# Convolution by FFT and mixture of experts on one core: inverse and unfolded loads in 64x64 tiles

## The chip, the cores and the metric

The kernel runs on one core of a Trainium2 chip. The metric is device microseconds of one execution, as the median of several runs. A profile is of one execution of its own, and its span is a little shorter than that execution's time.

## What is computed

For each of 8 sequences x of 5056 positions and 128 channels, a causal convolution with a filter h of the same length, channel by channel, written in the reference as a product of spectra of twice the length. Every row of the result then goes through a mixture of experts: a group of 4 by the largest logit, one of that group's 4 experts by the largest logit, two matrices with a ReLU between them, weighted by both softmax values.

```python
def _attn_ref(x, h):
    L = 2 * S
    Yf = np.fft.rfft(x, n=L, axis=1) * np.fft.rfft(h, n=L, axis=0)[None, :, :]
    return np.fft.irfft(Yf, n=L, axis=1)[:, :S, :]
...
            h = np.maximum(xg[mask_e] @ w1[g, e], 0.0)
            ye = h @ w2[g, e]
            out[tok_idx] = combined[:, None] * ye
```

## The kernel before

The transform of L = 10112 points is split into 158 x 64. A position is n1 * 64 + n2; only 79 of the 158 values of n1 hold data. All of this part is FP32, and the work goes in three rounds of three "units" each: h with sequences 0 and 1, then 2 to 4, then 5 to 7.

- **Stage 1** (`stage1`, L371) of a round does the 158-point transform over n1, for 79 frequencies. It takes 48 loads of 8 channels each: a tile of 80 partitions (79 rows of x and one of zeros, laid so that the even rows of n1 lie in partitions 24 to 63 and the odd ones in 64 to 103) by 512 elements. The matrix `f` is the moving operand, x the stationary one. Two of three loads are **folded** (L419): even and odd rows are transformed apart, in four 64x64 tiles of the array, to 40 frequencies (80 columns), and ACT and DVE make sum and difference of the two. Every third load (`i % 3 == 2`) is **unfolded** (L426): all 128 partitions as the contraction, two column tiles of 128x64, 158 columns, and ACT alone copies the result (L443). A step of the program is half a load, with a pair of PSUM banks for each load. When a load is done its tile becomes free and up to two new transfers are issued (L450), from SP in round 0 and from ACT's queue in the other rounds.
- **Groups** (`groups`, L463) take the 79 frequencies in 40 pairs `p`, two pairs to a step, 20 steps and a tail. `forward` (L503, matmuls L520) does the 64-point transform over n2 in 64x64 tiles; DVE multiplies with the spectrum of h (L538, twice a pair); POOL (round 0) or DVE (rounds 1 and 2) adds the two products (L572); `inverse` (L576, matmuls L587) does the 64-point inverse of an earlier step's pairs: four matmuls of a 64x128 tile each, `w` = 256 columns in round 0 and 384 in the others; ACT copies the result (L597) and SP stores it to `zd` in device memory.
- **Side** (`side`, L684) does the last 158-point inverse for a finished round (L721, L735), transposes (L778), the gating on DVE, and scatters rows, sorted by expert, through POOL. It runs woven into stage 1 and the groups of the next round, and for the last round into the experts.
- **Experts**: blocks of 512 rows through both matrices, each product as three matmuls of 512 columns on high and low parts (L1350 to L1352, L1368 to L1370).

The order on each engine is written out by the program: `weave` places the steps of the side between the main steps by weights. Each engine works its own queue in that order and waits on semaphores. The gating's running sums over an expert's tokens are one scan (L937) of a matrix of ones and zeros, `smask`, [128, 240] in FP32, which DVE writes twice in the program (L747).

Of the kernel before, what the change touches and what calls it, by code (L numbers as in the profile page):

```python
# [9 lines left out]
F32 = mybir.dt.float32  # L10
F32R = mybir.dt.float32r
BF16 = mybir.dt.bfloat16
# [8 lines left out]
N1, N2 = 158, 64  # L21
# [44 lines left out]
LP = 2  # L66
# [28 lines left out]
def dft_constants():  # L95
# [7 lines left out]
    f = np.zeros((128, N1))  # L103
    f[X0:X0 + NH + 1] = rows
# [108 lines left out]
def columns(nu):  # L213

    n = 8 * nu * NH
    t = (n + GP - 1) // GP
    return t, n - (t - 1) * GP
# [11 lines left out]
class Kernel:  # L229
# [33 lines left out]
    def setup(self):  # L263
# [11 lines left out]
        self.f = cp.tile([128, N1], F32, name="f")  # L275
        nc.sync.dma_start(out=self.f, in_=a["c_f"])

    def setup2(self):
# [74 lines left out]
        self.smask = cp.tile([128, NE * columns(3)[0]], F32, name="smask")  # L353
# [17 lines left out]
    def stage1(self, r):  # L371
# [21 lines left out]
        def load(eng=nc.sync):  # L393
            if asked[0] >= len(loads) or not free:
                return
            i = asked[0]
            asked[0] += 1
            u, q = loads[i]
            b = ROUNDS[r][u]
            src = a["h"] if b < 0 else a["x"][b]  # L400
            held[i] = t = free.pop(0)
            eng.dma_start(
                out=t[X0:X0 + NH + 1].rearrange("p (d n) -> p d n", n=N2), in_=src[:, 2 * q * QB:2 * (q + 1) * QB, :]
            )
            tiles[i] = t.rearrange("p (i h n) -> p i h n", h=2, n=N2)

        def mm(k):
            i, h = k // 2, k % 2
            u, q = loads[i]
            fold = i % 3 != 2  # L410
# [3 lines left out]
            whole = pp.rearrange("p b c -> p (b c)")  # L414
            for j in range(h * QB // 2, (h + 1) * QB // 2):
# [8 lines left out]
                else:  # L424
                    for c in range(2):
                        nc.tensor.matmul(  # L426
                            whole[c * 64:c * 64 + 64, j * 256:j * 256 + N1], lhsT=tiles[i][:, j, c, :], rhs=self.f,
                            start=True, stop=True, tile_position=(0, c * 64),
                        )
# [33 lines left out]
    def groups(self, r):  # L463
# [112 lines left out]
        def inverse(p):  # L576
# [7 lines left out]
            for part in range(2):  # L584
                for c in range(n):
                    wt, k = (cgs[p + LP], 320 - part * 64) if p > 0 else (first[0], part * 128)
                    nc.tensor.matmul(  # L587
                        pz[c][:, 0:w], lhsT=wt[c * 64:c * 64 + 64, k:k + 128],
                        rhs=y[c * 64:c * 64 + 64, part, 0:w], start=part == 0, stop=part == 1,
                        tile_position=(c * 64, 0),  # L590
                    )
# [1146 lines left out]
```

## Time and profile before

| | |
|---|---|
| median of 3 runs | 1703.45 us (1699.97 to 1713.07) |
| the profiled execution | 1699.58 us, span 1697.9 us |
| TensorE's granted clock | 0.993 of full speed |
| TensorE busy | 96% of the span |
| VectorE, ScalarE, GpSimd busy | 77, 62, 46% |
| stage 1 of rounds 0, 1, 2 | to 52.5 us, 156 to 216, 372 to 453 us |
| groups of rounds 0, 1, 2 | 52.5 to 156, 216 to 372, 453 to 612 us |

The page gives busy shares of the span, the span in 40 slices, the DMA queues and the costliest groups of instructions. The timeline lists instructions in order of time, neighbours of one kind merged, with the idle time ahead of them and what ended it; "issue" stands for a wait that nothing in the profile explains. Matmuls overlap and their ends are modelled, so the distance between two starts says what a piece takes. An FP32 matmul of the program is two records on TensorE, each with a weight load.

### The profile page before, as it was taken

What the parts mean: (1) busy time and instruction counts of PE and PEld (TensorE: products, weight loads), DVE (VectorE), ACT (ScalarE), POOL (GpSimd) and SP (SyncE); (2) the same over time, 40 slices, a digit from 0 to 9 for tenths busy, and PEclk for the clock granted to TensorE, in tenths of its full rate; (3) what the DMA queues carried; (4) which work ended last, traced back from release to release, by engine and by line L of the source; (5) the groups of instructions that cost most, each with busy time, mean ns of one, the idle gap of its engine ahead of it and who ended that gap; (6) DMA issues with size and microseconds to landing.
All of it is one profiled execution on the core that took longest, in us unless ns stands there. A gap on an engine that the chain in (4) does not pass through costs nothing. (4 is left out here: it accounts for less than half of the span.)

```text
span 1697.9 us, 49029 instructions
## 1 busy us (share of the span) xinstructions
PE 1637.9 (96%) x17369; PEld 1287.7 (76%) x17369; DVE 1302.8 (77%) x3092; ACT 1047.2 (62%) x2461; POOL 773.4 (46%) x742
## 2 busy tenths in 40 slices
PE   8998999998999989999999999999999999999997
PEld 7666766657766657888888887888888888878987
DVE  6554689885688886777777788888887788787876
ACT  4554544544454456666666676677777776666765
POOL 1353234342465553254544554355555664243444
PEclk9999999999999999999999999999999999999998
DMA  7688778878799976565565544457555674445455
GB/s 207 204 266 247 204 218 265 271 249 216 195 282 294 292 235 185 164 179 166 169 176 170 170 137 137 150 179 227 160 155 171 189 242 127 131 125 155 153 162 157
DMA packets 277993, 330.23 MB, mean 194 GB/s; under 512 B 31863, under 2 KB 210304, under 8 KB 277720
## 3 DMA queue, kind: packets, MB, share of 16 engines
q1 hardware_dynamic: 248856, 270.93, 54.2%
q0 software_dynamic: 20608, 41.79, 7.2%
q10 hardware_dynamic: 8256, 14.10, 3.1%
q8 instruction: 144, 2.36, 0.6%
q14 instruction: 129, 1.06, 0.2%
HBM read 230.35 MB, written 96.86 MB: 193 GB/s over the span
## 5 line engine op out<-in xcount | busy, mean ns | idle before, releaser
L854 POOL DMA_INDIRECT srt<-rw,pos x320 | 345.7, 1080 | 388.8 <-DVE pos L853 112.4
L1421 POOL DMA_INDIRECT out<-orow,at x176 | 187.8, 1067 | 253.8 <-ACT at L1419 226.3
L538 DVE TENSOR_TENSOR y<-pp,hg 128x768 f32<-128x768 f32 (+1 forms) x120 | 103.7, 864 | 60.3 <-ACT hg L528 37.1
L1421 POOL DMA_INDIRECT out<-orow,sids x92 | 93.8, 1020 | 121.8 <-DVE orow L1388 85.5
L597 ACT COPY zs<-pp 128x768 f32<-128x768 f32 (+1 forms) x118 | 85.1, 721 | 84.7 <-PE pp L587 52.1
L587 PE MATMUL pp<-y,cg 64*128 64x384 f32 (+1 forms) x736 | 120.2, 456 | 9.9 <-DVE m L538 8.1
L1356 DVE SCALAR_TENSOR_TENSOR h0l<-px,h0h 128x512 fp32r<-128x512 f32 (+1 forms) x109 | 73.6, 676 | 59.4 <-ACT h0h L1355 58.5
L520 PE MATMUL pp<-st,cg 64*64 64x192 f32 (+1 forms) x1556 | 115.3, 407 | 0.5 <-PE pp L587 0.4
L1355 ACT ACTIVATE h0h<-px 128x512 fp32r<-128x512 f32 (+1 forms) x109 | 63.9, 586 | 80.8 <-PE px L1352 72.7
L438 DVE TENSOR_TENSOR st<-pp,odd 128x320 f32<-128x320 f32 x96 | 46.9, 489 | 76.6 <-ACT odd L437 74.3
L538 DVE TENSOR_TENSOR m<-pp,hg 128x768 f32<-128x768 f32 (+1 forms) x120 | 102.9, 858 | 2.2 <-ACT hg L530 2.2
L587 PEld LDWEIGHTS pp<-y,cg 64*128 64x128 f32 x736 | 68.2, 187 | 46.6 <-issue 16.8
L1356 DVE SCALAR_TENSOR_TENSOR h2l<-px,h2h 128x512 fp32r<-128x512 f32 (+1 forms) x112 | 75.6, 675 | 31.1 <-ACT h2h L1355 30.0
L742 ACT COPY yT<-py 128x474 f32<-128x474 f32 (+1 forms) x96 | 44.5, 514 | 77.0 <-PE py L735 76.9
L1356 DVE SCALAR_TENSOR_TENSOR h3l<-px,h3h 128x512 fp32r<-128x512 f32 (+1 forms) x111 | 74.6, 672 | 22.5 <-ACT h3h L1355 21.0
L520 PEld LDWEIGHTS pp<-st,cg 64*64 64x64 f32 x1556 | 56.1, 132 | 45.3 <-issue 34.9
L572 POOL TENSOR_TENSOR y<-y,m 128x512 f32<-128x512 f32 x40 | 50.8, 1274 | 83.4 <-DVE m L560 44.8
L721 PEld LDWEIGHTS py<-ig,zm 126*64 126x64 f32 x2048 | 73.2, 137 | 19.4 <-issue 6.8
L721 PE MATMUL py<-ig,zm 126*64 126x79 f32 x2048 | 80.7, 234 | 4.1 <-ACT rw L779 2.8
L1355 ACT ACTIVATE h3h<-px 128x512 fp32r<-128x512 f32 (+1 forms) x111 | 65.2, 587 | 29.1 <-PE px L1352 24.1
L1356 DVE SCALAR_TENSOR_TENSOR h1l<-px,h1h 128x512 fp32r<-128x512 f32 (+1 forms) x111 | 74.7, 673 | 4.2 <-ACT h1h L1355 0.3
L1355 ACT ACTIVATE h1h<-px 128x512 fp32r<-128x512 f32 (+1 forms) x111 | 65.2, 588 | 17.1 <-PE px L1352 14.7
(476 smaller groups left out, 5153.5 us busy)
## 6 DMA issues: line engine op xcount, KB each, us to landing
wr<-in_moe_w SPq DMA_DIRECT2D x373, 256.0 KB
zd<-zs SPq DMA_DIRECT2D x78, 384.0 KB
zm<-zd SPq DMA_DIRECT2D x64, 378.0 KB
cg<-in_c_g SPq DMA_DIRECT2D x102, 224.0 KB
xr<-srt SPq DMA_DIRECT2D x71, 260.0 KB
hg<-hd SPq DMA_DIRECT2D x80, 128.0 KB
zd<-zs SPq DMA_DIRECT2D x39, 256.0 KB
xt<-in_x ACTq DMA_DIRECT2D x54, 160.0 KB
```

Of the source, the lines that this page charges most:

```text
L438: nc.vector.tensor_tensor(out=all_st[:, 0:2 * HALF, d], in0=even, in1=odd, op=ALU.add)
L520: nc.tensor.matmul(px[c * 64:c * 64 + 64, b, to], lhsT=k, rhs=data[:, of], start=begin, stop=i == len(steps) - 1 or p == 0 and i == 1, til ...
L538: nc.vector.tensor_tensor(out=t[:, :, 0:w].rearrange("p t (r u d) -> p t r u d", r=2, u=nu), in0=taken(px, part).unsqueeze(1).broadcast_to ...
L572: (nc.gpsimd if r == 0 else nc.vector).tensor_tensor(out=y[:, :, 0:w], in0=y[:, :, 0:w], in1=m[:, :, 0:w], op=ALU.add)
L587: nc.tensor.matmul(pz[c][:, 0:w], lhsT=wt[c * 64:c * 64 + 64, k:k + 128], rhs=y[c * 64:c * 64 + 64, part, 0:w], start=part == 0, stop=part ...
L597: nc.scalar.copy(out=z[:, 0:n, 0:w], in_=pp[:, 0:n, 0:w])
L721: nc.tensor.matmul(pys[q][c:c + 64, col(n, u)], lhsT=zms[q][:, n % QB, k:k + 64], rhs=self.ig[:, 0:NH], start=n % QB == 0 and u == 0, stop ...
L742: nc.scalar.copy(out=self.yT[:, k:k + QB * c1], in_=pys.pop(q)[:, 0:QB * c1])
L854: ins = self.nc.gpsimd.indirect_dma_start(out=self.srt, out_offset=bass.IndirectOffsetOnAxis(ap=k["pos"][0:p, j:j + 1], axis=0), in_=k["rw ...
L1355: nc.scalar.activation(out=hh, in_=p, func=AF.Relu)
L1356: nc.vector.scalar_tensor_tensor(out=hl, in0=p, scalar=0.0, in1=hh.bitcast(F32), op0=ALU.max, op1=ALU.subtract)
L1421: ins = self.nc.gpsimd.indirect_dma_start(out=self.a["out"], out_offset=bass.IndirectOffsetOnAxis(ap=ids, axis=0), in_=o, in_offset=None, ...
```

## The change

- The **inverse** is cut along its 128 output rows: eight matmuls of a 64x64 tile for a pair in place of four of 64x128, in the order of half `h`, then frequency `c`.
- An **unfolded load** comes as two transfers. Channels 0 to 3 of the load go to the array's first half, partitions 24 to 63, and channels 4 to 7 to the second, 64 to 103; in each half the even rows of n1 lie first along the free dimension, the odd rows behind them. The contraction over 80 rows becomes two accumulating matmuls over 40, in four 64x64 tiles.
- `f` gets 158 more columns: the even and odd rows' coefficients with the halves exchanged.
- `smask` is held in bfloat16.

```diff
-    f = np.zeros((128, N1))
-    f[X0:X0 + NH + 1] = rows
+    f = np.zeros((128, 2 * N1))
+    f[X0:X0 + NH + 1, 0:N1] = rows
+    f[X0:X0 + HALF, N1:] = rows[HALF:]
+    f[X0 + HALF:X0 + 2 * HALF, N1:] = rows[:HALF]
...
-        self.smask = cp.tile([128, NE * columns(3)[0]], F32, name="smask")
+        self.smask = cp.tile([128, NE * columns(3)[0]], BF16, name="smask")
...
+            if folded(i):
+                eng.dma_start(
+                    out=t[X0:X0 + NH + 1].rearrange("p (d n) -> p d n", n=N2),
+                    in_=src[:, 2 * q * QB:2 * (q + 1) * QB, :],
+                )
+            else:
+                for b in range(2):
+                    d = 2 * q * QB + b * QB
+                    eng.dma_start(
+                        out=t[X0 + b * HALF:X0 + (b + 1) * HALF].rearrange("p (s d n) -> p s d n", s=2, n=N2),
+                        in_=src[:, d:d + QB, :].rearrange("(s p) d n -> p s d n", s=2),
+                    )
...
+            if not fold:
+                for s in range(2):
+                    for c in range(2):
+                        for b in range(2):
+                            j = b * QB // 2 + h
+                            nc.tensor.matmul(
+                                whole[c * 64:c * 64 + 64, j * 256:j * 256 + N1],
+                                lhsT=tiles[i][b * 64:b * 64 + 64, s * QB // 2 + h, c, :],
+                                rhs=self.f[b * 64:b * 64 + 64, (b + s) % 2 * N1:(b + s) % 2 * N1 + N1],
+                                start=s == 0, stop=s == 1, tile_position=(b * 64, c * 64),
+                            )
...
-                else:
-                    for c in range(2):
-                        nc.tensor.matmul(
-                            whole[c * 64:c * 64 + 64, j * 256:j * 256 + N1], lhsT=tiles[i][:, j, c, :], rhs=self.f,
-                            start=True, stop=True, tile_position=(0, c * 64),
-                        )
...
             for part in range(2):
-                for c in range(n):
-                    wt, k = (cgs[p + LP], 320 - part * 64) if p > 0 else (first[0], part * 128)
-                    nc.tensor.matmul(
-                        pz[c][:, 0:w], lhsT=wt[c * 64:c * 64 + 64, k:k + 128],
-                        rhs=y[c * 64:c * 64 + 64, part, 0:w], start=part == 0, stop=part == 1,
-                        tile_position=(c * 64, 0),
-                    )
+                wt, k = (cgs[p + LP], 320 - part * 64) if p > 0 else (first[0], part * 128)
+                for h in (0, 64):
+                    for c in range(n):
+                        nc.tensor.matmul(
+                            pz[c][h:h + 64, 0:w], lhsT=wt[c * 64:c * 64 + 64, k + h:k + h + 64],
+                            rhs=y[c * 64:c * 64 + 64, part, 0:w], start=part == 0, stop=part == 1,
+                            tile_position=(c * 64, h),
+                        )
```

The order of the engines' work stays; the number of instructions in its pieces changes. On TensorE at the start of stage 1 of round 0 (`pp` is the pair of PSUM banks, `xt` a tile of x, `f` the matrix; the shape is the output's, x16 the number of matmuls), before:

```order
L419 MATMUL pp<-f,xt_80 64x80 x16
L419 MATMUL pp<-f,xt_81 64x80 x16
L426 MATMUL pp<-f,xt_82 64x158 x8
L419 MATMUL pp<-f,xt_83 64x80 x16
L419 MATMUL pp<-f,xt_84 64x80 x16
L426 MATMUL pp<-f,xt_80 64x158 x8
```

and now:

```order
L444 MATMUL pp<-f,xt_80 64x80 x16
L444 MATMUL pp<-f,xt_81 64x80 x16
L434 MATMUL pp<-f,xt_82 64x158 x16
L444 MATMUL pp<-f,xt_83 64x80 x16
L444 MATMUL pp<-f,xt_84 64x80 x16
L434 MATMUL pp<-f,xt_80 64x158 x16
```

Every third load has 16 matmuls for 8; the others are as they were.

On TensorE in the groups of round 0, the second and third steps (`st` is stage 1's result, `cg` and `ns` the transform's matrices, `y` the product), before:

```order
L520 MATMUL pp_1166<-st_95,cg_909 64x384 x4
L520 MATMUL pp_1166<-st_95,cg_909 64x192 x4
L520 MATMUL pp_1166<-st_95,ns_1139 64x192 x4
L587 MATMUL pp_1191<-y_1106,first_716 128x256 x4
L587 MATMUL pp_1200<-y_1129,cg_909 128x256 x4
L520 MATMUL pp_1212<-st_95,cg_959 64x384 x4
```

and now:

```order
L539 MATMUL pp_1310<-st_95,cg_1024 64x192 x4
L539 MATMUL pp_1310<-st_95,ns_1283 64x192 x4
L607 MATMUL pp_1335<-y_1250,first_800 64x256 x8
L607 MATMUL pp_1348<-y_1273,cg_1024 64x256 x8
L539 MATMUL pp_1364<-st_95,cg_1079 64x384 x4
L539 MATMUL pp_1364<-st_95,cg_1079 64x192 x4
```

The inverse stands at its place with eight matmuls for four, of 64 output rows.

On ACT's queue in stage 1 of round 1 (`odd` and `st` are its copies out of PSUM, DMA rows the loads that it issues), before:

```order
L443 COPY st<-pp 128x158x4
L402 DMA xt_81<-in_x 80x512
L437 COPY odd<-pp 128x320
L402 DMA xt_82<-in_x 80x512
L437 COPY odd<-pp 128x320
L402 DMA xy<-in_x 80x512
```

and now:

```order
L462 COPY st<-pp 128x158x4
L412 DMA xt_81<-in_x 40x2x256 x2
L456 COPY odd<-pp 128x320
L405 DMA xt_82<-in_x 80x512
L456 COPY odd<-pp 128x320
L405 DMA xy<-in_x 80x512
```

An unfolded load is two commands of 40 partitions for one of 80, at the same place.

More of the change, by code (lines that the diff above doesn't have):

```diff
@@ L274, in setup @@
             nc.vector.memset(t, 0.0)
-        self.f = cp.tile([128, N1], F32, name="f")
+        self.f = cp.tile([128, 2 * N1], F32, name="f")
         nc.sync.dma_start(out=self.f, in_=a["c_f"])
@@ L401, in load, with folded @@
             held[i] = t = free.pop(0)
-            eng.dma_start(
-                out=t[X0:X0 + NH + 1].rearrange("p (d n) -> p d n", n=N2), in_=src[:, 2 * q * QB:2 * (q + 1) * QB, :]
-            )
+            if folded(i):
[10 more added lines that the diff above has]
+                    )
             tiles[i] = t.rearrange("p (i h n) -> p i h n", h=2, n=N2)
+        def folded(i):
+            return i % 3 != 2
         def mm(k):
@@ L409, in mm @@
             u, q = loads[i]
-            fold = i % 3 != 2
+            fold = folded(i)
             if h == 0:
@@ L584, in inverse @@
             for part in range(2):
-                for c in range(n):
-                    wt, k = (cgs[p + LP], 320 - part * 64) if p > 0 else (first[0], part * 128)
-                    nc.tensor.matmul(
-                        pz[c][:, 0:w], lhsT=wt[c * 64:c * 64 + 64, k:k + 128],
-                        rhs=y[c * 64:c * 64 + 64, part, 0:w], start=part == 0, stop=part == 1,
-                        tile_position=(c * 64, 0),
-                    )
+                wt, k = (cgs[p + LP], 320 - part * 64) if p > 0 else (first[0], part * 128)
[6 more added lines that the diff above has]
+                        )
             z = cx.tile([128, 2, W], F32, name="zs", bufs=3)
```

## The prediction

> **What bounds the kernel now.** I read the page's busy times first, then the table of stretches, cut where the matmul lines change (stage 1 of the three rounds, their groups, the change-over, the experts), then TensorE's timeline inside a stretch of each kind.
>
> ```profile
> PE 1637.9 (96%) x17369; PEld 1287.7 (76%) x17369; DVE 1302.8 (77%) x3092; ACT 1047.2 (62%) x2461; POOL 773.4 (46%) x742
> ```
>
> ```profile
> 0.00:52.50 52.50, 44.02 (x1280) 37.85 (x1280) 31.72 (x93) 25.86 (x50) 6.45 (x23) 1.00 0.67 192
> 52.50:156.00 103.50, 100.75 (x1508) 69.80 (x1508) 56.74 (x95) 57.33 (x169) 54.91 (x48) 1.00 0.82 252
> 156.00:216.30 60.30, 53.74 (x1490) 44.60 (x1490) 33.80 (x120) 29.37 (x67) 10.10 (x10) 1.00 0.76 197
> 216.30:372.00 155.70, 149.04 (x2117) 92.71 (x2116) 139.85 (x333) 73.07 (x198) 59.49 (x54) 1.00 0.81 257
> 372.00:453.50 81.50, 74.60 (x1893) 60.75 (x1893) 48.76 (x202) 38.63 (x84) 33.35 (x38) 0.96 0.83 219
> 453.50:612.00 158.50, 154.91 (x2384) 100.72 (x2386) 139.80 (x337) 77.41 (x214) 93.13 (x86) 1.00 0.87 273
> 640.00:1000.00 360.00, 357.73 (x3113) 289.51 (x3114) 273.66 (x637) 244.17 (x591) 167.61 (x159) 1.00 0.59 168
> ```
>
> Columns: stretch, length, busy time and instructions of PE, PEld, DVE, ACT, POOL, then granted clock, DMA share, GB/s. PE sets the pace: 97% busy in the first groups, 96 and 98% in the next two, 99% with the experts. So what is won or lost before 612 us shifts everything behind it by as much. Two things limit that. In the groups of rounds 1 and 2 DVE is at 90 and 88% and the DMA engines at 0.81 and 0.87. And stage 1 (rows 1, 3, 5) is the loosest: PE is idle for 8.5, 6.6 and 6.9 us there, although DVE, ACT and POOL are all under 61%.
>
> **The inverse in 64x64 tiles.** TensorE's timeline in the first groups (start, length, line, form, records; one FP32 matmul of the program leaves two records):
>
> ```profile
> 65.50 1.20 PE L520 MATMUL pp<-st,cg 64*64 64x384 f32 x16
> 66.52 0.51 PE L520 MATMUL pp<-st,ns 64*64 64x192 f32 x8
> 66.85 1.15 PE L520 MATMUL pp<-st,cg 64*64 64x384 f32 x16
> 67.82 0.51 PE L520 MATMUL pp<-st,ns 64*64 64x192 f32 x8
> 68.25 2.00 PE L587 MATMUL pp<-y,cg 64*128 64x256 f32 x16
> 70.18 1.20 PE L520 MATMUL pp<-st,cg 64*64 64x384 f32 x16
> ```
>
> Lengths overlap, so I use differences of starts. L520 already runs in 64x64 tiles, four at once. Its x16 piece (8 records of 384 columns, 8 of 192) streams 2 x 384 + 2 x 192 = 1152 columns from 66.85 to 67.82: 0.97 us, 0.84 ns a column. The x8 piece streams 384 in 0.33 (66.52 to 66.85): 0.86. L587, in 64x128 tiles two at once, streams 8 x 256 = 2048 columns in 1.93 us (68.25 to 70.18): 0.94 ns. In 64x64 tiles it has twice the records, four at once, so the same 2048 columns: 1.72 to 1.76 us, 0.19 us less a step of two pairs. The change of tile shape goes too: the L520 piece ahead of L587 takes 0.43 instead of 0.33 (67.82 to 68.25), and the one behind it 1.02 instead of 0.97. Together 0.34 us a step, 20 steps: **6.8 us** in round 0.
>
> Rounds 1 and 2 have 384 columns:
>
> ```profile
> 605.50 0.50 PE L520 MATMUL pp<-st,ns 64*64 64x192 f32 x8
> 605.94 2.85 PE L587 MATMUL pp<-y,cg 64*128 64x384 f32 x16
> 608.72 0.98 PE L778 MATMUL py<-ident,yT 128*128 128x128 f32 x7
> ```
>
> 8 x 384 = 3072 columns in 2.78 us (0.905 ns) become 2.58 to 2.64: 0.17 us a step. The shape change costs 0.11 ahead (605.50 to 605.94, against 0.33) and 0.05 behind, but only where no other matmul stands between, as L778 does here. From 0.17 (never) to 0.33 (always) I take the middle, 0.25, for 40 steps: **10 us**.
>
> How much arrives? In round 0 no other engine is over 55% and DMA is at 0.82: 6 of 6.8. In the other rounds DVE has work for 90% of the time, and what ends its waits is PE:
>
> ```profile
> L538 DVE TENSOR_TENSOR y<-pp,hg 128x768 f32<-128x768 f32 x32 | 30.5, 952 | 9.1 <-PE pp L520 9.1
> ```
>
> (240 to 360 us.) A faster PE first shortens those 9.1 us, then meets DVE and, in round 2, DMA. With 5 us less in 156 DVE would be at 93%: I count 3.5 of 5 in round 1, 3 in round 2. Sum for the groups: **-12.5 us**, bounds -5 (two queues near full) and -20 (all of it, shape changes always).
>
> **The unfolded loads.** Stage 1 of round 0, late part:
>
> ```profile
> 39.95 0.56 PE L419 MATMUL pp<-f,xt 64*64 64x80 f32 x18 [1.60 <-issue]
> ...
> 44.56 0.36 PE L419 MATMUL pp<-f,xt 64*64 64x80 f32 x6 [0.95 <-issue]
> 44.85 1.29 PE L426 MATMUL pp<-f,xy 128*64 128x158 f32 x16
> 46.08 1.34 PE L419 MATMUL pp<-f,xt 64*64 64x80 f32 x64
> 47.34 1.29 PE L426 MATMUL pp<-f,xy 128*64 128x158 f32 x16
> 48.57 0.64 PE L419 MATMUL pp<-f,xt 64*64 64x80 f32 x23
> 49.61 0.37 PE L419 MATMUL pp<-f,xt 64*64 64x80 f32 x9 [0.40 <-issue]
> ```
>
> An unfolded load (L426) is 8 x 158 = 1264 columns in 1.23 us (47.34 to 48.57). In four tiles that is 1.06 to 1.09 us at L520's price, or 1.24 at the 0.984 ns of the 80-column folds (1280 columns from 46.08 to 47.34). 158 is nearer to 192: 1.09, and 0.05 for the shape change. So 0.19 us less a load, 9 us for 48 loads (bounds 0 and 10), if PE's work is what stage 1 waits for. I hold that it is not.
>
> **Where that gain goes.** The stalls above stand in the middle of a load, behind nothing but "issue": no data, no buffer. From 44.56 to the next stall PE starts 6 + 16 + 64 + 16 + 23 = 125 records. The queue that carries instructions, on the whole page and in the three stretches of stage 1:
>
> ```profile
> q8 instruction: 144, 2.36, 0.6%
> ```
>
> ```profile
> q8 instruction: 10, 0.16, 1.3%
> ...
> q8 instruction: 13, 0.21, 1.7%
> ...
> q8 instruction: 14, 0.23, 1.3%
> ```
>
> 144 packets of 16 KB for 17369 matmuls and as many weight loads: one packet per 121 matmuls; in the stretches 1280/10, 1490/13, 1893/14, so 115 to 135. PE thus stops where a packet ends and the next is not there. Two packet-bound stalls in a row end 4.61 us (39.95 to 44.56) and 5.05 us (to 49.61) after the one before. PE's work for 125 records is 2.49 us per 80 (46.08 to 48.57, two folded loads and an unfolded one), 3.9 us. PE and packets are nearly level today:
>
> ```profile
> PE pp L419 <- issue: 10.5, 11, 2.8
> ```
>
> (all waits of this kind: total, times, longest). The change makes 32 records out of 16 for each unfolded load: 96 per three loads in 2.30 us, 125 in 3.0 us. Each round gets 256 matmul records and 256 weight loads more, 2 packets. A packet that takes over 3.0 us now holds PE up. In round 0, at 4.61 us a packet, 2.05 more packets cost 9.4 us. With the loads spread over a longer time the DMA engines (0.67 now) are freer, and some packets must have come within 3.9 us, since only some end in a stall: I take +5. In rounds 1 and 2 other matmuls (L721, L778) stand between, packets were used at 60.3/13 = 4.6 and 81.5/14 = 5.8 us each: +4 each. Stage 1 in sum: **+13 us**, bounds -9 (every packet in time) and +28 (6.1 packets at 4.61).
>
> In the groups a step of 64 records in 4.68 us (65.50 to 70.18) becomes 80 in 4.34, 125 in 6.8 us: longer than a packet takes, so no loss there.
>
> The rule against this: the Trainium skill ("Runtime: NRT & Kernel Launch", "Instruction fetch mechanics") has instructions arrive in 16 KiB blocks of 256 while the engine works on the block before, and calls the cost of a boundary mostly hidden. The trace agrees with the block (125 matmuls and as many weight loads between stalls) and not with the hiding (waits of up to 2.8 us). By the rule stage 1 would give the full -9 and the forecast would be the first rival.
>
> **What costs nothing.** Transfers (queue: packets, MB, share), a transfer's command on ACT's queue, and the scan (least, median and longest ns):
>
> ```profile
> q1 hardware_dynamic: 248856, 270.93, 54.2%
> q10 hardware_dynamic: 8256, 14.10, 3.1%
> ```
>
> ```profile
> 172.11 0.32 ACTq L402 DMA_DIRECT2D xy<-in_x  x1
> ...
> L937 DVE TENSOR_TENSOR_SCAN cs<-smask,oh x24: 477/654/659, 184.9 to 1001.1; 128x240 f32<-128x240 f32 x16, 128x160 f32<-128x160 f32 x8
> ```
>
> An unfolded load is now two transfers with runs half as long. q10 (2 KB runs) costs 3.1% x 16 x 1697.9 / 8256 = 102 ns for 1.7 KB, q1 59 ns for 1.1 KB: the same per KB. ACT issues one more 0.32 us command per unfolded load in rounds 1 and 2, 10 us in all under an engine that is 47 to 49% busy. It stands behind the copy out of PSUM; the next copy waits for it. I count +0.5, at most +4. The bfloat16 mask is read by 24 scans of 0.65 us off PE's path, and written twice: nothing (bounds -1 and +1).
>
> **Sum.** -12.5 + 13 + 0.5 = +1 us, on a profiled execution of 1699.58 (span 1697.9). The median of the runs, 1703.45 us, is 3.9 above that execution; I carry the difference over: **1704 us**, no change that the measurement would tell (1% is 17 us, 1686 to 1720).
>
> **The rivals.**
> - *The packets come in time.* For it: 11 such waits of L419 stand against 37 packets in the three stretches, so most come in time today. Against it: 125 records would have to be fetched every 3.0 us, and the measured pace of stalled packets is 4.61 to 5.05. Then -9 in stage 1 and about -15 in the groups: 1703 - 24 = 1680 us, faster. Chance 0.16.
> - *Stage 1 runs at the packets' pace throughout.* If PE asks for a packet only when it enters the one before, then with 3.0 us of work in each every packet is late, and all 6.1 cost 4.61 us: +28, with -10 from the groups 1703 + 18 = 1721 us, slower. The sum turns to slower from 1.6 us for each added packet on (10 over 6.1), and passes 1% at 4.4 (27 over 6.1). For it: the two intervals of 4.61 and 5.05; against it: rounds 1 and 2 have slower matmuls between. Chance 0.12.
> - *The groups are held by DVE and DMA* (90% and 0.87): only -5 there, 1703 + 13 - 5 + 0.5 = 1712, within 1%. Chance 0.1.
> - *The tiles don't go four at once* in the inverse, since here the two that share a row half are not neighbours in the order: then the price stays near 0.94 ns, the groups give only the shape changes, -4, and the end is as in the rival before. Chance 0.04.
>
> My forecast has 0.58. Faster by over 1% 0.16, within 1% 0.7 (0.58 + 0.1 + 0.02 of the last rival, which may also end slower), slower 0.14. The range of 8 in 10 reaches down to half of what the first rival adds and up to the second: 1686 to 1719; the forecast's own range is 1694 to 1713.
>
> **What would show it.** Right: the start of round 0's groups later than 52.5 us (about 57), more "issue" waits in stage 1 than 10.5 us, 12 packets instead of 10 there, an inverse step of 1.72 to 1.76 us in round 0 and 2.6 in the others, groups of round 0 shorter by some 6 us. Wrong: stage 1 shorter than before with stalls no longer than now (first rival); stage 1 longer by over 8 us in each round (second); inverse pieces still 1.93 and 2.78 long (last). A profile in which the groups' gain is gone while PE waits for L538 or for cg would be the third.

## The result and the profile after

The changed kernel took 1717.04 us (median of 8 runs, 1706.84 to 1722.69), the kernel before 1703.62 beside it (8 runs, 1699.66 to 1714.79). The ratio is 1.006, 95% interval 1.0039 to 1.0081: slower by 6.6 to 13.8 us, within the 1% that was forecast as no change. It is 13 us above the forecast's 1704, outside the forecast's own range (1694 to 1713) and 2 us inside the wide one (1686 to 1719). The profiled execution took 1717.78 us, span 1716.0, mean granted clock 0.984 (before 0.993).

First the page, then the table of stretches of the changed kernel, cut at its own marks: the first matmul of each round's groups and of the next stage 1, and the first of the experts. Columns as in the prediction.

```profile
PE 1633.1 (95%) x19085; PEld 1286.4 (75%) x19085; DVE 1302.6 (76%) x3092; ACT 1044.2 (61%) x2461; POOL 772.0 (45%) x742
```

```profile
0.00:57.20 57.20, 40.61 (x1536) 38.12 (x1536) 31.84 (x93) 24.91 (x50) 6.47 (x23) 1.00 0.62 178
57.20:144.80 87.60, 85.83 (x1578) 60.44 (x1578) 52.25 (x84) 51.80 (x158) 49.85 (x40) 1.00 0.87 272
144.80:224.10 79.30, 67.44 (x1997) 57.52 (x1997) 38.15 (x130) 33.57 (x77) 15.05 (x19) 0.89 0.65 180
224.10:375.20 151.10, 143.99 (x2362) 85.38 (x2360) 136.14 (x319) 70.97 (x194) 56.82 (x52) 1.00 0.81 258
375.20:469.60 94.40, 79.33 (x2218) 66.91 (x2217) 52.42 (x216) 39.99 (x90) 35.91 (x40) 0.91 0.75 199
469.60:640.30 170.70, 161.49 (x2732) 98.82 (x2730) 151.58 (x368) 82.48 (x226) 99.13 (x92) 0.98 0.87 270
```

Three of these stretches in the kernel before, at its own marks (stage 1 of round 1, groups of rounds 1 and 2):

```profile
145.80:216.40 70.60, 62.56 (x1730) 51.71 (x1730) 38.29 (x130) 34.35 (x77) 14.94 (x19) 1.00 0.75 201
216.40:368.30 151.90, 146.29 (x2058) 90.92 (x2056) 136.39 (x319) 71.53 (x194) 56.96 (x52) 1.00 0.81 256
453.50:624.20 170.70, 163.22 (x2420) 104.55 (x2418) 151.50 (x368) 82.76 (x226) 99.78 (x92) 0.98 0.86 268
```

By these marks stage 1 of round 1 begins at 145.8 us and that of round 2 at 368.3. The 156 and 372 us ahead of the prediction, at which its rows are cut too, are late.

The same cuts at the marks of the kernel before, in its first trace and in a second one (e8 below), give this table of lengths in us:

| stretch | before | before again | after | after less before | forecast |
|---|---|---|---|---|---|
| stage 1, round 0 | 52.6 | 52.0 | 57.2 | +4.6 | +5 |
| groups, round 0 | 93.2 | 93.3 | 87.6 | -5.6 | -6 |
| stage 1, round 1 | 70.6 | 70.6 | 79.3 | +8.7 | +4 |
| groups, round 1 | 151.9 | 152.3 | 151.1 | -0.8 | -3.5 |
| stage 1, round 2 | 85.2 | 88.9 | 94.4 | +9.2 | +4 |
| groups, round 2, and change-over | 170.7 | 170.3 | 170.7 | 0.0 | -3 |
| experts | 1073.7 | 1076.7 | 1075.7 | +2.0 | 0 |

The reader is to see three things. PE is busy for 4.8 us less (1637.9 before), and the span is 18.1 longer. Round 0 did what was forecast in both stages. Stage 1 of rounds 1 and 2 lost twice the forecast, at a granted clock of 0.89 and 0.91 (1.00 and 0.96 before), and their groups gained almost nothing. The column "before again" says how far one execution may be trusted: stage 1 of round 2 moves by 3.7 us and the experts by 3.0 without any change, so of the 18.1 us between these two traces the ratio confirms 10. Stage 1 of round 0 took 52.0 to 54.2 us in the six traces that run it with the matmuls of before, and 56.9 to 59.1 in the four with the change's.

**Round 0, stage 1.** TensorE's timeline of the changed kernel (L444 folded, L434 unfolded; in brackets the idle time before):

```profile
50.67 1.20 PE L444 MATMUL pp<-f,xt 64*64 64x80 f32 x57 [1.99 <-issue]
51.69 1.25 PE L434 MATMUL pp<-f,xy 64*64 64x158 f32 x32
52.77 0.73 PE L444 MATMUL pp<-f,xt 64*64 64x80 f32 x32
53.32 0.30 PE L444 MATMUL pp<-f,xy 64*64 64x80 f32 x5
54.62 0.70 PE L444 MATMUL pp<-f,xy 64*64 64x80 f32 x26 [1.00 <-issue]
```

From 50.67 to the next stall PE starts 57 + 32 + 32 + 5 = 126 records, in 3.95 us with the stall: the packet again. It can be counted more closely. Over all rows that the trace has on TensorE's queue (matmuls, weight loads and semaphore rows), each of the nine "issue" stalls of this stage stands exactly 256 rows behind the one before it. Of the 38 "issue" waits in stage 1 of rounds 1 and 2 of e9 and e10 (below), 34 stand on the same grid of 256. So these waits are waits at the end of a packet. An unfolded load takes 1.08 us (51.69 to 52.77), the 1.09 of the prediction without its 0.05 for the shape. "Issue" waits of this stretch sum to 10.7 us (3.6 before), and it has two packets more, 12:

```profile
q8 instruction: 12, 0.20, 1.6%
```

**Round 0, groups.** The same step as in the prediction's second timeline:

```profile
67.63 0.51 PE L539 MATMUL pp<-st,ns 64*64 64x192 f32 x8
67.96 1.91 PE L607 MATMUL pp<-y,cg 64*64 64x256 f32 x32
69.69 1.15 PE L539 MATMUL pp<-st,cg 64*64 64x384 f32 x16
```

The inverse now takes 1.73 us (67.96 to 69.69; 1.93 before), and the L539 piece ahead of it 0.33 (67.63 to 67.96; 0.43 before). In 18 steps of this round an inverse has L539 on both sides.

**Rounds 1 and 2, groups.** TensorE's timeline at the same two steps of round 1, of the changed kernel and of the kernel before:

```profile
289.16 2.81 PE L607 MATMUL pp<-y,xt 64*64 64x384 f32 x32
291.79 1.15 PE L539 MATMUL pp<-st,cg 64*64 64x384 f32 x16
...
296.44 2.81 PE L607 MATMUL pp<-y,cg 64*64 64x384 f32 x32
299.19 0.44 PE L798 MATMUL py<-ident,yT 128*128 128x128 f32 x2
```

```profile
281.44 2.85 PE L587 MATMUL pp<-y,xt 64*128 64x384 f32 x16
284.22 1.20 PE L520 MATMUL pp<-st,cg 64*64 64x384 f32 x16
...
288.92 2.85 PE L587 MATMUL pp<-y,cg 64*128 64x384 f32 x16
291.70 0.44 PE L778 MATMUL py<-ident,yT 128*128 128x128 f32 x2
```

Where a 64x64 piece follows, the inverse takes 2.63 us now, 2.78 before. Where the 128x128 transposes follow, 2.75 against 2.78: a change of shape on the way out takes most of the gain. On the way in nothing is won in these two steps, since other matmuls stand ahead of the inverse (the transposes, and L755 of 32x64; in the kernel before L778 and L735), and the last of them takes as long as before, 0.53 and 0.70 us to the inverse's start. Counted in the trace, of the 20 inverses in each of these rounds 5 and 6 stand directly behind L539 (the piece ahead then takes 0.32 us for 0.44), and 4 and 3 directly ahead of it (2.63 for 2.78); behind all the others another matmul follows, and the whole ones of these take 2.74 for 2.78. By these prices the tiles are worth about 2 us a round, and PE is busy for 2.3 and 1.7 us less (146.29 to 143.99, 163.22 to 161.49). Even that does not arrive: the groups are 0.8 and 0.0 us shorter. In the four full kernels with this inverse (the change, e5, e9, e10) round 1's take 150.9 to 153.0 us, against 151.9 and 152.3 before.

The largest group of lines of the inverse in round 1, after and before (busy us, mean ns, then idle time before):

```profile
L607 PE MATMUL pp<-y,cg 64*64 64x384 f32 x432 | 39.0, 488 | 5.2 <-DVE m L557 4.9 <-DVE off L995 0.2
```

```profile
L587 PE MATMUL pp<-y,cg 64*128 64x384 f32 x216 | 40.0, 500 | 4.1 <-DVE m L538 4.0 <-DVE off L975 0.2
```

It is busy for 1.0 us less, and PE waits 0.9 us more ahead of it for DVE's `m`.

**Rounds 1 and 2, stage 1.** Here the stalls are of another kind. PE's "issue" waits in stage 1 of round 1 fell, from 3.9 to 1.6 us; its waits for ACT and DVE rose from 3.1 to 9.8. TensorE's timeline there, and under it ACT with the commands on its queue (ACTq):

```profile
154.60 0.78 PE L444 MATMUL pp<-f,xt 64*64 64x80 f32 x32 [0.96 <-DVE st L458]
156.76 2.38 PE L434 MATMUL pp<-f,xt 64*64 64x158 f32 x32 [1.38 <-ACT st L462]
159.15 1.34 PE L444 MATMUL pp<-f,xt 64*64 64x80 f32 x32
```

```profile
149.86 1.43 ACTq L405 DMA_DIRECT2D xt<-in_x  x1
151.42 0.42 ACT L456 COPY odd<-pp 128x320 f32<-128x320 f32 x1 [0.87 <-PE pp L444]
151.44 1.60 ACTq L412 DMA_DIRECT2D xt<-in_x  x2
153.16 0.42 ACT L456 COPY odd<-pp 128x320 f32<-128x320 f32 x1 [1.32 <-DVE st L458]
155.65 0.34 ACTq L405 DMA_DIRECT2D xt<-in_x  x1
156.02 0.69 ACT L462 COPY st<-pp 128x632 f32<-128x632 f32 x1 [2.44 <-DMA zt<-zd]
```

ACT is done with its copy at 153.58 and does nothing until 155.65, when a load's command may go; the copy `st` (156.02) stands behind it, and PE, which needs the PSUM that `st` empties, starts L434 at 156.76. It then runs at half speed: 2.39 us to the next piece where a load took 1.08 in round 0. Half speed is the larger part of this stage's loss. PE is busy for 67.4 us here, and for 61.8 and 61.6 in e9 and e10 (below), which run the same matmuls in this stage at a granted clock of 1.00; so some 5.7 us of the 8.7 are matmuls at the lower clock. PE's idle time grew by 3.8 us (8.0 to 11.9).

The commands of round 1's stage 1 by line, after and before (count, then least, median and longest ns):

```profile
L405 ACTq DMA_DIRECT2D xt<-in_x x16: 334/335/1487, 148.9 to 207.3; - x16
L405 ACTq DMA_DIRECT2D xy<-in_x x12: 334/335/748, 159.0 to 207.8; - x12
...
L412 ACTq DMA_DIRECT2D xt<-in_x x22: 294/328/583, 145.8 to 209.5; - x22
L412 ACTq DMA_DIRECT2D xy<-in_x x8: 307/308/388, 162.4 to 206.7; - x8
```

```profile
L402 ACTq DMA_DIRECT2D xt<-in_x x27: 318/318/1402, 146.8 to 200.7; - x27
...
L402 ACTq DMA_DIRECT2D xy<-in_x x16: 318/319/783, 155.9 to 200.1; - x16
```

58 commands for 43. They hold the queue for 23.8 us (15.5 before), and ACT's waits that end with a transfer's landing rose from 4.9 to 14.6 us (round 2: 3.8 to 15.6).

What such a command waits for is seen in the program's order with the semaphores that each row waits for (ACT, start of stage 1 of round 1, the changed kernel):

```
198 L405 DMA xt_81<-in_x 80x512 [waits DMAHW2_49]
199 L462 COPY st<-pp 128x158x4 [waits PE_49]
200 L405 DMA xt_82<-in_x 80x512 [waits DMAHW5_49]
201 L456 COPY odd<-pp 128x320 [waits DVE_49,PE_49,Activation_49]
202 L412 DMA xt_83<-in_x 40x2x256 [waits DMAHW7_49]
203 L412 DMA xt_83<-in_x 40x2x256 [waits DMAHW0_49]
```

In this program every transfer that SP or ACT issues takes one of eight semaphores, DMAHW0 to 7, in turn (the trace has 1299 such commands, 161 to 164 for each of the eight), and waits until the transfer that held it eight places earlier has landed, whichever queue that was on. So a load's command can end its wait with SP's `zt<-zd`. Stage 1 of round 1 has 95 such commands now (58 on ACT, 37 on SP) and 80 before: the ring of eight turns faster.

### The profile page after: what moved, and what is told of

Its sections match the earlier page's. It is cut to its first block, busy times and chain, and to the rows that moved or that the text cites. A ratio compares the mean times of both kernels' runs of the same rounds, so it can differ in the third digit from the quotient of the medians.

```text
span 1716.0 us, 52520 instructions
## 1 busy us (share of the span) xinstructions
PE 1633.1 (95%) x19085; PEld 1286.4 (75%) x19085; DVE 1302.6 (76%) x3092; ACT 1044.2 (61%) x2461; POOL 772.0 (45%) x742
## 5 line engine op out<-in xcount | busy, mean ns | idle before, releaser
L617 ACT COPY zs<-pp 128x768 f32<-128x768 f32 (+1 forms) x118 | 85.2, 722 | 84.2 <-PE pp L607 48.8
L607 PE MATMUL pp<-y,cg 64*64 64x384 f32 (+1 forms) x1472 | 116.3, 443 | 11.1 <-DVE m L557 8.4
L539 PE MATMUL pp<-st,cg 64*64 64x192 f32 (+1 forms) x1556 | 114.6, 404 | 1.6 <-issue 0.7
L741 PEld LDWEIGHTS py<-ig,zm 126*64 126x64 f32 x2048 | 78.4, 144 | 23.7 <-issue 7.9
L607 PEld LDWEIGHTS pp<-y,cg 64*64 64x64 f32 x1472 | 55.4, 133 | 51.2 <-issue 27.8
L741 PE MATMUL py<-ig,zm 126*64 126x79 f32 x2048 | 86.7, 243 | 6.4 <-ACT rw L799 3.7
L539 PEld LDWEIGHTS pp<-st,cg 64*64 64x64 f32 x1556 | 59.1, 133 | 40.8 <-issue 32.3
L591 POOL TENSOR_TENSOR y<-y,m 128x512 f32<-128x512 f32 x40 | 50.8, 1274 | 82.2 <-DVE m L579 49.1
L1376 DVE SCALAR_TENSOR_TENSOR h1l<-px,h1h 128x512 fp32r<-128x512 f32 (+1 forms) x111 | 74.7, 673 | 3.9
L1375 ACT ACTIVATE h1h<-px 128x512 fp32r<-128x512 f32 (+1 forms) x111 | 65.2, 587 | 16.5 <-PE px L1372 14.6
```

Of the source, the lines that this page charges most:

```text
L539: nc.tensor.matmul(px[c * 64:c * 64 + 64, b, to], lhsT=k, rhs=data[:, of], start=begin, stop=i == len(steps) - 1 or p == 0 and i == 1, til ...
L591: (nc.gpsimd if r == 0 else nc.vector).tensor_tensor(out=y[:, :, 0:w], in0=y[:, :, 0:w], in1=m[:, :, 0:w], op=ALU.add)
L607: nc.tensor.matmul(pz[c][h:h + 64, 0:w], lhsT=wt[c * 64:c * 64 + 64, k + h:k + h + 64], rhs=y[c * 64:c * 64 + 64, part, 0:w], start=part = ...
L617: nc.scalar.copy(out=z[:, 0:n, 0:w], in_=pp[:, 0:n, 0:w])
L741: nc.tensor.matmul(pys[q][c:c + 64, col(n, u)], lhsT=zms[q][:, n % QB, k:k + 64], rhs=self.ig[:, 0:NH], start=n % QB == 0 and u == 0, stop ...
L1375: nc.scalar.activation(out=hh, in_=p, func=AF.Relu)
```

## The experiments

Theory from the profile of the changed kernel: the loss of stage 1 is the records (packets) in round 0, and ACT's doubled commands in rounds 1 and 2. Rivals: records and packets in all rounds; the four tiles themselves; the inverse.

Kernels e1 to e4 ran in a session in which the kernel before took 1792.39 us; the same chip gave 1704.95 for it beside e5. Why is not known, and rounds 1 and 2 are stretched in these traces (stage 1 of e1: 82 and 107 us). So of e1 to e4 only ratios and lengths of round 0 are used, and the ratios hold for that session.

**e1, the inverse alone.** The kernel before with the change's inverse:

```diff
-                        pz[c][:, 0:w], lhsT=wt[c * 64:c * 64 + 64, k:k + 128],
+                        pz[c][h:h + 64, 0:w], lhsT=wt[c * 64:c * 64 + 64, k + h:k + h + 64],
```

> The kernel before with the inverse alone in 64x64 tiles; loads, f and mask as before. Theory (the inverse is a gain, the unfolded loads a loss by their instruction packets): stage 1 of round 0 ends at 52.5 us as before, the groups of round 0 take about 5.5 us less, those of rounds 1 and 2 at most 1 us less each; in all 5 to 8 us under before, about 1697. Rival (the packets of the inverse's added instructions cost what its tiles win): groups of round 0 no shorter, total within 2 us of before.

Ratio 0.9987 (0.9963 to 1.0011). Round 0's groups took 87.4 us, their stage 1 54.1. There the inverse is worth at most 0.37% (6 us of 1700); the forecast's 12.5 is outside. Stage 1 of round 0, which e1 leaves as it was, is within the spread given above.

**e2, the loads alone.** The change without the inverse's hunk.

> The change without its inverse: unfolded loads in 64x64 tiles by two transfers, mask in bfloat16, inverse in 64x128 tiles. Theory: groups of round 0 start near 57 us, stage 1 of rounds 1 and 2 some 8 us longer each, no gain in the groups: 18 to 24 us over before, about 1724, more than the whole change. Rival (the inverse's instructions make part of the loss): about 1710, under the whole change.

Ratio 1.0124 (1.0085 to 1.0162); stage 1 of round 0 56.9 us, its groups 93.3. The loads carry the whole loss: more than the change itself, as its theory said.

**e3 and e12, the change's loads with matmuls in 64x128 tiles.** Transfers, commands and mask of the change, 16 records a load as before; e12 is the same kernel again, beside a kernel before at 1704.0 us:

```diff
-                    for c in range(2):
-                        for b in range(2):
...
+                    for b in range(2):
...
+                            whole[:, j * 256:j * 256 + N1],
+                            lhsT=tiles[i][b * 64:b * 64 + 64, s * QB // 2 + h].rearrange("p c n -> p (c n)"),
```

> The two transfers, the wide f and the bfloat16 mask of the change, but the unfolded load in 64x128 tiles: as many matmuls as before the change (8 a load), two at a time, each half of the array with 40 rows. Inverse as before. Theory (the count of instructions decides, transfers cost nothing): stage 1 of round 0 ends near 52.5 us and the total is within 4 us of before. Rival (the doubled transfers, their runs of 1 KB or the added commands on ACT decide): stage 1 of all rounds as long as with the whole change, total 15 us or more over before.

> The kernel before, with the change's loads and mask, the unfolded matmuls in 64x128 tiles (two at once, 16 records a load as before), and the inverse in 64x128 tiles as before. Theory of the commands: stage 1 of round 0 as before, 52 to 53 us with 10 packets; stage 1 of rounds 1 and 2 still 4 to 9 us longer each, since the commands are the change's; total 1712 to 1720 us. Rival (the records and packets of the four tiles lengthen stage 1 in all rounds): 52, 71 and 86 us, total 1702 to 1707 us.

e3: ratio 1.0043 (1.0017 to 1.007), stage 1 of round 0 52.4 us. e12: 1717.0 us, 4 runs, ratio 1.008 (1.0049 to 1.011); stage 1 51.4, 73.8 and 91.6 us (before 52.6, 70.6, 85.2), packets 10, 14 and 15 as before. Without the added records round 0 loses nothing; rounds 1 and 2 lose 3.2 and 6.4 all the same (2.7 in round 2 against the second trace of before). The round 1 figure is below the 4 expected. The total is about as long as the change's, without its gain in round 0's groups and without its packets. So the packets are round 0's cause, and not the only one in the others. (These kernels take the four tiles away together with the records; that it is the records, and not the tiles, the 256 rows between the stalls say.)

**e4, the unfolded matmuls in one 128x128 tile.** The kernel before, transfer and all, with one matmul in place of two:

```diff
-                    for c in range(2):
-                        nc.tensor.matmul(
-                            whole[c * 64:c * 64 + 64, j * 256:j * 256 + N1], lhsT=tiles[i][:, j, c, :], rhs=self.f,
+                    nc.tensor.matmul(
+                        whole[:, j * 256:j * 256 + N1], lhsT=tiles[i][:, j].rearrange("p c n -> p (c n)"),
```

> The kernel before with the unfolded load in one tile of 128x128: 4 matmuls a load for 8, the same columns streamed, one transfer. Theory (packets): one packet less in each round's stage 1, so round 0's groups start 2 to 4 us before 52.5, rounds 1 and 2 gain as much, fewer waits without a cause in stage 1, total 6 to 12 us under before, about 1694. Rival (PE's work in stage 1 decides, which is the same here): no change, 1703, round 0's groups at 52.5.

Ratio 0.9974 (0.9945 to 1.0003); stage 1 of round 0 49.1 us. Half the records of an unfolded load, 3.5 us less: the packets' price also shows in the other direction.

**e5, e1 and e4 together.**

> The inverse in 64x64 tiles together with the unfolded load in one 128x128 tile (4 matmuls a load, one transfer, f and mask as before). Theory: the two gains add, since one lies in the groups and one in stage 1: round 0's groups start near 49 us and last near 87.5, total 0.3 to 0.7% under before. Rival (DVE and DMA set the pace from round 1 on, so that an earlier start is given back): round 0 as said, total within 0.2% of before.

1698.78 us (8 runs, 1694.98 to 1702.6) against 1704.95, ratio 0.9965 (0.9953 to 0.9978): faster than both kernels. Stage 1 49.4, 70.1 and 86.8 us, 9 packets in round 0, and in its stage 1 the "issue" waits are nearly gone (0.4 us; 3.6 before). That is the low end of the theory's 0.3 to 0.7%. The gain lies in round 0 (3.2 us in stage 1, 5.2 in the groups); rounds 1 and 2 show none (groups 151.9 and 171.9 us).

**e6 and e7, is it DVE that keeps the groups' gain?** e6 is the kernel before without the addition in rounds 1 and 2; e7 is e6 with the change's inverse. Their routing changes, so only the groups are compared. Each ran once.

```diff
-            (nc.gpsimd if r == 0 else nc.vector).tensor_tensor(
+            if r == 0:
+                nc.gpsimd.tensor_tensor(
```

> The kernel before without DVE's addition of the two products in rounds 1 and 2 (the inverse takes the first product alone, so rows are routed otherwise and the experts' time is not to be compared). It is the base for the next run. Theory (DVE holds the groups of rounds 1 and 2): they are shorter than before by some us, with PE busy near 100%. Rival (DMA holds them): as long as before, with PE idle for as much as now.

> The run before with the inverse in 64x64 tiles, the same addition left out. Theory (DVE kept the inverse's gain from arriving in rounds 1 and 2): with DVE relieved the groups of rounds 1 and 2 are 3 to 6 us shorter than in the run before, as those of round 0 are. Rival (something else, DMA or the order of the work, keeps it): they differ by less than 1.5 us.

The groups of rounds 1 and 2 in the table of stretches, e6 then e7:

```profile
218.30:366.90 148.60, 145.15 (x2060) 90.98 (x2056) 104.00 (x279) 70.74 (x194) 51.11 (x53) 1.00 0.83 262
454.40:620.20 165.80, 160.04 (x2420) 103.59 (x2419) 117.00 (x326) 82.16 (x226) 90.11 (x92) 1.00 0.87 274
```

```profile
213.70:360.30 146.60, 143.44 (x2363) 85.54 (x2360) 103.83 (x279) 70.82 (x194) 50.93 (x53) 1.00 0.84 266
447.30:612.30 165.00, 158.21 (x2731) 98.50 (x2730) 116.64 (x326) 82.51 (x226) 90.32 (x92) 1.00 0.89 275
```

With 32 us of DVE's work gone (136.4 to 104.0 in round 1) the groups are 3.3 and 4.9 us shorter than before (151.9, 170.7), so DVE does hold them in part. The inverse then gains 2.0 and 0.8 us, against 0.8 and 0.0 with the addition. DVE thus hid about 1 us a round, hardly clear of the scatter of single traces. The other 7 of the 10 us forecast were never there, as the count of neighbours says.

**e8, the kernel before again,** for a second trace.

> The kernel before once more, for a trace on the same chip as these runs. Every theory expects the stages of its first trace: groups of round 0 from 52.5 us on, 93 us long.

1705.89 us; its lengths are in the first table.

**e9, one command a load, the records of the change.** The rows of those channels are laid ahead in the tile's order, so that one transfer of 80 runs brings a load:

```diff
-                for b in range(2):
-                    d = 2 * q * QB + b * QB
-                    eng.dma_start(
...
+            eng.dma_start(
+                out=t[X0:X0 + NH + 1].rearrange("p (d n) -> p d n", n=N2), in_=src[:, 2 * q * QB:2 * (q + 1) * QB, :]
+            )
```

> The changed kernel, with the rows of the unfolded loads' channels laid out ahead in the order of the tile, so that each unfolded load is again one transfer of 80 runs of 2 KB with one command, as before; the matmuls, their tiles and their number are those of the change. Theory of the commands (stage 1 of rounds 1 and 2 is lengthened because ACT's commands double for the unfolded loads, ACT waits in them, and TensorE then waits for ACT's copies until its clock halves): stage 1 of round 0 stays near 57 us (12 packets), stage 1 of round 1 comes back from 79 to 71 to 74 us and of round 2 from 94 to 85 to 89 us, waits of ACT ended by its own transfers fall from 14.6 and 15.6 to about 5 us each, the half-clock time there goes to 0 to 7 us, and the total is 1703 to 1706 us. Rival (more records and packets, or the four tiles themselves, lengthen these stages): 79 and 94 us stay, half-clock time stays, 1714 to 1720 us.

**e10, the two commands from SP.**

```diff
-                    eng.dma_start(
+                    nc.sync.dma_start(
```

> The changed kernel, with the two commands of an unfolded load issued from SP's queue in all rounds, where the change takes ACT's in rounds 1 and 2. Theory of the commands: with two thirds of the load commands left on ACT and one each, ACT's waits ended by its own transfers fall to about 3 us a round, stage 1 of rounds 1 and 2 is 71 to 76 and 85 to 90 us, the total 1703 to 1708 us. Rival (packets and records): 79 and 94 us stay, 1714 to 1720. A second rival: on SP the commands stand behind SP's own waits for free buffers, the loads come late and TensorE waits for them; then stage 1 is longer than 79 and 94 us with waits ended by a load.

**e11, two commands a load, the records of before.**

```diff
+            parts = 2 if i % 3 == 2 else 1
+            for k in range(parts):
+                w = 2 * QB // parts
...
+                eng.dma_start(out=td[:, k * w:(k + 1) * w, :], in_=src[:, d:d + w, :])
```

> The kernel before, with each unfolded load split into two transfers of 80 runs of 1 KB (one command each, halves of its channels); the matmuls are those of before. It adds the change's commands and its runs, and none of its records. Theory of the commands: stage 1 of round 0 stays at 52 to 53 us (SP issues there), stage 1 of rounds 1 and 2 is longer by 4 to 9 us each with ACT's waits for its own transfers above 10 us, the total 1710 to 1720 us. Rival (packets and records): within 2 us of before, 1702 to 1707 us.

Beside a kernel before at 1704.0 us (26 runs): e9 1714.63, 9 runs, ratio 1.007 (1.0047 to 1.0093). e10 1713.14, 10 runs, 1.0041 (1.0019 to 1.0062). e11 1711.73, 10 runs, 1.0046 (1.0026 to 1.0065). Neither theory comes through whole. The commands' one has e11 (+7.8 us where the packets' said within 2 of before) and e10's round 1 (72.5 us). The packets' one has e9's total and round 2 of both e9 and e10. What they have in common stands in the waits. Stage 1 of rounds 1 and 2, in us: its length, and two kinds of PE's waits in it, summed (its waits for transfers, 0.2 to 3.7 us, are left out):

| kernel | more records | more commands on ACT | round 1: length, issue, ACT + DVE | round 2: length, issue, ACT + DVE |
|---|---|---|---|---|
| before | no | no | 70.6, 3.9, 3.1 | 85.2, 6.3, 0 |
| before again | no | no | 70.6, 3.5, 2.9 | 88.9, 6.6, 3.0 |
| e5 | fewer | no | 70.1, 1.4, 2.7 | 86.8, 6.3, 1.8 |
| e11 | no | yes | 74.7, 1.8, 4.9 | 89.4, 3.8, 6.9 |
| e12 | no | yes | 73.8, 1.9, 6.5 | 91.6, 3.9, 8.7 |
| e9 | yes | no | 75.7, 10.3, 3.2 | 94.9, 12.8, 0 |
| e10 | yes | no (on SP) | 72.5, 7.5, 3.3 | 94.5, 13.2, 0 |
| after | yes | yes | 79.3, 1.6, 9.8 | 94.4, 4.7, 9.6 |

More commands on ACT: PE waits for ACT and DVE (in e11's round 1 also 3.7 us for transfers, 1.2 before), and the "issue" waits shrink. More records: PE waits for packets, and the others stay as before. With both, the first kind stands and the second is all but gone from the list; as I read it, the packets come in while PE stands still for ACT.

In round 1 each alone lengthens the stage, the records by 1.9 and 5.1 us (e10, e9) and the commands by 3.2 and 4.1 (e12, e11), and both by 8.7. In round 2 the records add 5.6 to 9.7 us; the 0.5 to 6.4 of the commands are not set apart from the 3.7 between the two traces of before, and both add 5.5 to 9.2, no more than the records alone. In total the records with the inverse cost 11.9 us (e9), the commands 7.8 (e11), and both with the inverse 10.2 (the change), not 19.7. With e10's 7.0 in place of e9's the sum would be 14.8, which the intervals do not tell from 10.2. So the two cover each other in part, and by how much stays open. The first theory, commands alone in rounds 1 and 2, falls; the waits in the trace of after name only the one that came last.

Stage 1 of round 1 of e9, and PE's largest waits in it:

```profile
144.80:220.50 75.70, 61.80 (x1994) 53.12 (x1994) 38.08 (x130) 33.84 (x77) 15.49 (x20) 1.00 0.67 188
PE pp L435 <- issue: 8.8, 7, 3.0
PE py L732 <- issue: 1.5, 2, 1.3
```

and ACT's commands of e11 there, to set beside L402's above:

```profile
L407 ACTq DMA_DIRECT2D xt<-in_x x38: 318/335/1767, 147.9 to 206.3; - x38
L407 ACTq DMA_DIRECT2D xy<-in_x x20: 318/334/1431, 159.3 to 204.3; - x20
```

The same loads, the same bytes, and the queue is held for 25.8 us where it was 15.5. e11's transfers also have shorter runs, but so have e10's, and there PE's waits for ACT and DVE stay as before. Nor did the loads take longer in the changed kernel: their queue, q10, was busy for 31.5% of 79.3 us on 16 engines, 400 us for 7.05 MB, and before for 36.3% of 70.6, 410 us.

Left open: why e10's round 1 is 3.2 us shorter than e9's. e9's ACT still waits 12.7 us for transfers in round 1, with 43 commands; PE, late by its packets there, did not wait for it. How the clock shares in round 2's loss is not separated from the waits that set it off. A program with more than eight semaphores was not tried, so that the ring is what holds the commands is read from the program, not shown by a run.

## Why the prediction was right, and where it was wrong

- **Stage 1 of round 0, +5:** right, by its own mechanism. 12 packets, 57.2 us, stalls after 126 records, +4.6. e3 and e12 take the added records back and the loss is gone; e4 and e5 have half the records of before and the stage falls under its old length. The Trainium skill's "mostly hidden" ("Runtime: NRT & Kernel Launch", "Instruction fetch mechanics") is not borne out in this stream: 10.7 us of 57.2.
- **Groups of round 0, -6 of 6.8:** right, -5.6, with the inverse at 1.73 us (1.72 to 1.76 forecast), so four tiles do go at once.
- **Groups of rounds 1 and 2, 0.25 us a step, "10 us", of which 3.5 and 3 arrive:** the term was mis-sized. The price per column held (2.63 us for 3072 columns, forecast 2.58 to 2.64), and so did the prices of a change of shape from and to L539 (0.12 ahead, 0.05 behind). What failed was the middle between "never" and "always": only a quarter of the inverses stand next to L539 on a side (5 and 6 of 20 behind it, 4 and 3 ahead of it). And "never", 0.17, was not the least: where another shape follows, the inverse in small tiles pays for that change and gains 0.03 to 0.04. That makes some 4 us for the two rounds in place of 10. DVE, named as what would hold it, hid about 2 us in all (e6, e7). -0.8 in sum for -6.5.
- **Packets in rounds 1 and 2, +4 each:** the mechanism was right. Where the records act without more commands on ACT, round 1 is +5.1 and +1.9 (e9, e10), on both sides of the forecast, and round 2 +5.6 to +9.7 against the two traces of before, above it; e9's and e10's round 2 has 20.5 and 13.7 us of half clock in it (6.8 before). In the changed kernel's round 1 other waits took its place. The pace was read from rows cut late: at the right marks it is 70.6/14 = 5.0 and 85.2/15 = 5.7 us a packet, which changes little.
- **The commands on ACT, "+0.5, at most +4":** the step that failed. It priced 0.32 us a command and let it disappear under an engine that is 47 to 49% busy. Alone they cost 7.8 us (4.4 to 11.1; e11). The busy share of ACT's copies says nothing of its queue: a command waits there for another transfer's landing, for up to 2.4 us in the lines above, and the copy behind it is the one that PE waits for. The 10 us that the prediction names before it hides them was the better number: 7.8 us over the 30 commands added in these stages is 0.26 each.
- **The clock** stood in no term. Half speed took 17.1 us of stage 1 in each of rounds 1 and 2 (0 and 6.8 before). In round 1 that is some 5.7 of the 8.7 us lost: the waits set it off, and it costs more than they do.
- **The mask:** nothing, as forecast. 24 scans at a median of 652 ns (654 before), two writes of 258 ns in both kernels.

So the class was right and the point 13 us low. The class was right with help from its width, since both large errors, in the groups and in stage 1, went the same way: by the two profiled executions, 6.1 us too much gain in the groups, 9.4 too little loss in stage 1 of rounds 1 and 2, 2.0 in the experts that the kernel before shows by itself, less 0.4 in round 0. Of the rivals, the first (packets in time) and the fourth (not four at once) are refuted by round 0. The second is not what happened, though rounds 1 and 2 passed its mark of 8 us: they did so with fewer "issue" waits than before. Its total, 1721, is nearer to the measured 1717 than the forecast's 1704 all the same, by terms that it did not name. The third rival's -5 for the groups is near the measured -6.4, but for another reason than its own: the neighbours in the order, and DVE only for about 2 us.

## What to carry to other kernels

Count records and commands as well as columns: where a stretch of short matmuls ran at about a packet per 4 us, as here, a tiling with twice the records for the same columns lost more than it gained, and one with half the records (e5) won. Count how often the pieces whose price you compare are really neighbours. Do not take a command as hidden because the copies of its queue fill only half of the time; ask which copy stands behind it and who waits for that. Price the clock that a wait sets off, not only the wait. And when a change adds two waits, do not read their sizes from the trace of the change: the larger hides the other, and only runs with one of them at a time tell.

## What the runs showed of the hardware

**The clock falls by short waits that add up.** Rows of e9, cut at a place where the granted clock falls and where it comes back:

```profile
397.00:400.30 3.30, 2.29 (x93) 2.27 (x97) 1.39 (x6) 0.91 (x2) 1.40 (x2) 1.00 1.03 237
400.30:403.66 3.36, 1.33 (x38) 1.07 (x37) 0.94 (x3) 0.54 (x2) 2.59 (x3) 1.00 0.94 284
403.66:413.90 10.24, 9.72 (x180) 7.96 (x180) 2.44 (x12) 2.45 (x5) 2.29 (x3) 0.50 0.60 156
```

PE was idle for 2.0 of 3.36 us and then had half the clock for 10.24 us, three times 3.41. All stretches of half clock that end within a trace are multiples of 3.41 us on one grid. I laid PE's idle time from 10 to 650 us on that grid in six traces (before, after, e9 to e12). Of the windows that ran at full clock themselves, all 18 with 1.95 us or more idle were followed by half clock, none of the 977 with less than 1.0 was, and of the 85 between 10 were. The Trainium skill ("TensorE: Matmul & The Clock Gate", "HAM oscillation — how this bites in real kernels") gives as the rule that no idle gap should exceed about 3.4 us. Here waits that add up to 2 us within one such window were enough, so that rule is too wide for this kernel. The sums per window fit that 10.3 us of packet stalls spread over e9's round 1 (at most 1.74 us in a window) left the clock at 1.00, and that 9.8 us of waits for ACT and DVE in the changed kernel, in a few places (2.31, 2.02 and 1.85 us in a window), did not.

**Tile shapes have a price per change,** on leaving as on entering: 0.12 us more for an inverse of 3072 columns in 64x64 tiles when 128x128 pieces follow (2.75 against 2.63 us), as 0.11 more for a 64x64 piece of L520 ahead of an inverse in 64x128 tiles (0.44 against 0.33 us).
